# Reordering two seams of a long-convolution and token-mixing kernel: three phase steps ahead of the last inverse, plain products first in the second pass

## The chip, the cores and the metric

The kernel runs on one core of a Trainium2 chip. The metric is the device time of one execution in microseconds. Before the change it was 2134.84 us, the median of three runs (2129.86 to 2135.28).

## What is computed

Two steps follow each other. The first is a causal convolution of `x` (8 batches, 5696 positions, 128 channels) with a filter `h` of the same length. The second turns each value into a real and an imaginary part by a learned phase, mixes all positions with two 5696 x 5696 matrices, and ends in a small layer over the channels.

```python
L = 2 * S
y = irfft(rfft(x, n=L, axis=1) * rfft(h, n=L, axis=0), n=L, axis=1)[:, :S, :]
theta = y @ w_theta
zr, zi = y * cos(theta), y * sin(theta)
m = einsum('ts,bsd->btd', w_tok_r, zr) + einsum('ts,bsd->btd', w_tok_i, zi)
u = y + m
out = u + maximum(u @ w_ch, 0.0)
```

## The kernel before

**Convolution.** Batches go in pairs and channels in halves, which makes eight groups. Each group runs a forward transform (`stage_a`, `stage_b`) and an inverse (`stage_c`, `stage_d`); the forward part of one group is woven with the inverse of the one before (the loop at L594). `stage_b` writes the products with the filter's spectrum into `u_t` and `v_t` (L307), for which it loads filter chunks `hs` from HBM (L298). `stage_c` multiplies from these two tiles (L323, L324) and evacuates to `g`; `stage_d` multiplies `g` (L346), evacuates to `yt` on ScalarE (L349), and stores to `yt_hbm` (L355). For the last group the first half of `yt` is also copied straight into the tile `ya1` by SP (`load_ya1`, L549), and the rest is stored by GpSimd.

**Phase steps.** `phase_step` (L556) takes 128 positions of half the batches. It transposes them on TensorE (L569), forms the phase in PSUM (L399 to L405), copies the transposed values (L574), takes an absolute value and two sines on ScalarE (L410 to L412), multiplies twice on VectorE (L423, L424), and stores the values to `y2_hbm` (L575) and the two parts `zz` to `z_hbm` (L441) or straight into a `b` tile (L437). There are 22 steps for the first half of the batches (`steps0`) and 22 for the second (`steps1`). Of the first 22, ten are woven into the last group's `stage_c`, six into its `stage_d`, and six follow. Six of the woven steps also release one weight load each (`with_load`).

**Mixing.** Positions 0 to 5631 of both sides are cut in four halves of 2816. A pass `p` takes one half of the source positions. Within a pass, a pair `tt` of 128-row tiles is multiplied with the source tiles `b` in stretches of three (the source half is 11 tiles `j`, so a pair has four stretches: tiles 0 to 2, 3 to 5, 6 to 8, and 9 and 10). Most pairs use seven products in place of eight, as in Strassen's scheme (L1060), which needs sums of the `b` tiles (`sum_ops`, L642, five per tile) and of the weights (`w_sum`, L711). A few pairs use the eight plain products instead (L982), which need neither; `plain(p, tt)` names them. The pair called `None` is the last 64 rows (L934, L936), here "the short pair". The order of the pairs is the list `pairs` (L447): in the first pass the short pair stands next to last, in the second pass it stands first.

**Weights.** GpSimd loads the mixing matrices in chunks into a ring of six slots (`load_w`, L501); each load is four DMAs. `ring["upto"]` holds how far the loads may go, and `pump` issues them when a slot has been read. VectorE transposes each chunk into a `wt` tile (L702, `w_t`). `prepare(i + 1)` emits the transposes and sums of the next stretch ahead of the products of this one. At the end of a pair they are given out in steps between the products (`woven`), if the next pair isn't the short one.

**Order.** The instructions are put into a queue for each engine by a planner that follows program order and expected readiness; `tc.issue_after(x)` keeps the enclosed instructions behind `x` on the same engine. In two regions VectorE keeps the written order (`manual_schedule`, L894): at the start of each pass, up to `(0, 2, 6)` and up to `(1, 1, 0)`.

**Start of the passes.** For the first pass `b` tiles 0 to 8 are filled in part from `z_hbm` (L639) and in part straight from the phase steps; tiles 9 and 10 are loaded by SP in `open_mixing` (L680). The first stretches (`i == 1`) are interleaved with `steps1`, one step after every second piece. The values that a pair's result is added to, `cs`, come from `addend` (L801): for the first pass from `y2_hbm` (L814) or `yt_hbm` (L810), by SP, and for the first pair they are loaded behind the last `b` tile (`sides["late"]`). For the second pass `start_pass(1)` loads all eleven `b` tiles through ScalarE's queue (L628), each as soon as the last pair of the first pass has read its tile, and adds two small tiles `zl` (L835). Results of the second pass go through an output stage, `u_stage` (L773): transposes (L782), a product (L789) and a last VectorE operation (L791). `aside` gives these stages out, one per stretch, in two parts.

Of the kernel before, what the change touches and what calls it, by code (L numbers as in the profile page):

```python
# [22 lines left out]
def kernel(  # L23
# [310 lines left out]
    def stage_d(st, bp, dh, then=None):  # L334
        def chunk(n0, cn):
            if n0 == 0:
                st["yt"] = fg.tile([P, NB, N2], BF16, tag="yt", name="yt")
            g_, yt = st["g"], st["yt"]
            ps = psum()
            nq = 5 if cn == CN else cn  # L340
            for j in range(cn):
                n = n0 + j
                o = ps[:, j // nq, (j % nq) * NB:(j % nq + 1) * NB]
                for ri in range(2):
                    e_ = e_t[:K1, n, ri, :] if n < EN else e_t[:K1, N2 - n, ri, ::-1]
                    nc.tensor.matmul(o, g_[:K1, ri * N2 + n, :], e_, start=(ri == 0), stop=(ri == 1))  # L346
            y_out = yt[:, :, n0:n0 + cn].rearrange("p m (a q) -> p m a q", q=nq)
            y_in = ps[:, :cn // nq, :nq * NB].rearrange("p a (q m) -> p m a q", q=nq)
            nc.scalar.activation(y_out, y_in, AF.Copy)  # L349
            if n0 + cn == N2:  # L350
                if then is not None:
                    then(yt)
                for e in range(2):
                    t0 = H if then else 0
                    (nc.gpsimd if then else nc.sync).dma_start(  # L355
                        yt_hbm[dh * HD:(dh + 1) * HD, 2 * bp + e, t0:],
                        yt[64 * e:64 * e + 64].rearrange("p m n -> p (m n)")[:, t0:])
        return [lambda n0=n0, cn=cn: chunk(n0, cn) for n0, cn in CHN]

    zz_n, ZB = [0], 3  # L360
# [312 lines left out]
    def open_mixing():  # L673
# [170 lines left out]
    def prepare(i, at_once=True):  # L844
# [45 lines left out]
    nxt, second, st = None, None, {}  # L890
    ordered = ExitStack()
    for i, (k, p, tt, j0, s0, nj) in enumerate(stretches):
        if (p, tt, j0 + s0) in ((0, 0, 0), (1, None, 0)):
            ordered.enter_context(tc.manual_schedule(engines={mybir.EngineType.DVE}))  # L894
        elif (p, tt, j0 + s0) in ((0, 2, 6), (1, 1, 0)):
            ordered.close()
# [18 lines left out]
        a, nxt = nxt, None if i == 1 else prepare(i + 1, not woven)  # L915
        if woven:
            nxt, step = nxt
        if tt is None:


            if first_of_pair:
                ps = [mps.tile([P, 512], F32, tag=f"m{q}", name=f"m{q}") for q in ((M2, M6) if p else (M3, M4))]
                cs = [addend(p, h, NT - 1, h, m=64) for h in range(2)]
            a1, a2, sa = a
            terms = (((a1, M2, a2, M7), (a1, M6, a2, M5)) if sa is None else
                     ((sa, M2, a2, M4), (a1, M3, sa, M5)))
            for j in range(nj):
                jj = j0 + s0 + j
                for r in range(2):
# [3 lines left out]
                    for h, (x0, q0, x1, q1) in enumerate(terms):  # L933
                        nc.tensor.matmul(ps[h][:64], x0[:, j, :64, r], b[q0],  # L934
                                         start=st_, stop=False)
                        nc.tensor.matmul(ps[h][:64], x1[:, j, :64, r], b[q1],  # L936
                                         start=False, stop=sp_)
            if p == 1:
# [13 lines left out]
            continue  # L952
        classic = plain(p, tt)
        if first_of_pair and i:
            ms = [mps.tile([P, 512], F32, tag=f"m{q}", name=f"m{q}") for q in (range(7) if not classic else (M7, M5, M1, M3) if p else (M2, M6, M1, M7))]
# [10 lines left out]
        def aside(first_of, second_of):  # L966
            nonlocal second
            if first_of and spread and (p == 1 or (tt > 0 and not end_of_pair)):
                where_bg["tags"] = ("c2", "c3") if j0 + s0 == TJ else ("red", "mag")
                _, first, second = spread.pop(0)  # L970
                with tc.issue_after(sides["late"].ins) if p == 0 and tt == 1 else ExitStack():
                    first()
                    if len(spread) > 1:
                        spread[1][0]()
            if second_of and second is not None:
                second()
                second = None

        def product(a, jj, j, n, hs):
            for r in range(2):  # L980
# [29 lines left out]
        if classic:  # L1010
# [112 lines left out]
```

## Time and profile before

| | |
|---|---|
| runs, median of three | 2134.84 us (2129.86 to 2135.28) |
| profiled execution, its own time | 2127.44 us |
| its span, first to last instruction | 2125.3 us |
| mean granted TensorE clock | 0.971 |
| VectorE, ScalarE, GpSimd busy | 75%, 32%, 43% |
| L1060, a Strassen product of 512 columns | 379 ns each, 1600 and 160 of them |
| L702, a transpose of a weight chunk | 523 ns each, 720 of them |
| L501, a weight DMA issued by GpSimd | 550 ns each, 1440 of them |

A group of the profile is one line of the kernel with its engine, operation and tile. A time for one instruction runs from its start to its end, and matmuls overlap, so the pace of TensorE is read from the starts. "Idle before" is the time that an engine waited ahead of an instruction, and the releaser is what ended the wait. The DMA share is the mean busy share of the core's 16 DMA engines, and it can stand above 1 where transfers overlap.

### The profile page before, as it was taken

What the parts mean: (1) busy time and instruction counts of PE and PEld (TensorE: products, weight loads), DVE (VectorE), ACT (ScalarE), POOL (GpSimd) and SP (SyncE); (2) the same over time, 40 slices, a digit from 0 to 9 for tenths busy, and PEclk for the clock granted to TensorE, in tenths of its full rate; (3) what the DMA queues carried; (4) which work ended last, traced back from release to release, by engine and by line L of the source; (5) the groups of instructions that cost most, each with busy time, mean ns of one, the idle gap of its engine ahead of it and who ended that gap; (6) DMA issues with size and microseconds to landing.
All of it is one profiled execution on the core that took longest, in us unless ns stands there. A gap on an engine that the chain in (4) does not pass through costs nothing.

```text
span 2125.3 us, 41308 instructions
## 1 busy us (share of the span) xinstructions
PE 1984.6 (93%) x15587; PEld 1112.7 (52%) x15765; DVE 1593.7 (75%) x2880; ACT 674.6 (32%) x997; POOL 908.1 (43%) x1661
## 2 busy tenths in 40 slices
PE   4788889787999999999999998999999999999998
PEld 3787888754444444444444443444444444444444
DVE  7767767776778888888886757677777777686867
ACT  5777877883232323332310000011111111111111
POOL 5301011237344536354556543444444454545450
PEclk8699999999999999999999999999999999999999
DMA  6457464989789989898999879777878787969693
GB/s 141 100 130 171 128 161 132 230 249 231 159 154 179 174 177 166 172 174 174 176 174 158 138 145 268 108 140 140 147 134 150 129 155 129 157 123 158 125 157 90
DMA packets 408264, 334.95 MB, mean 158 GB/s; under 512 B 85927, under 2 KB 358439, under 8 KB 407079
## 3 DMA queue, kind: packets, MB, share of 16 engines
q0 software_dynamic: 225952, 156.72, 52.1%
q1 hardware_dynamic: 176128, 164.05, 26.7%
q10 hardware_dynamic: 5984, 11.54, 1.5%
q8 instruction: 123, 2.02, 0.4%
q14 instruction: 77, 0.63, 0.1%
HBM read 377.11 MB, written 92.49 MB: 221 GB/s over the span
## 4 chain that ended last, share of the span: by engine, by line
PE 64%; DMA 3%; DVE 3%; issue 1%; POOL 1%; ACT 0%; DVEq 0%; ACTq 0%; POOLq 0%
PE m L1060 57%; PE m L982 2%; DMA b<-z_hbm 2%; DVE c L1067 1%; PE v L789 1%; PE utp L782 1%; POOL ring L501 1%; PE m L1064 1%; DVE wt L702 1%; DMA ring<-in_moe_w_tok_r_dram 1%; PE m L936 0%; PE m L934 0%; PE theta_ps L388 0%; PE tpz L730 0%; DMA ring<-in_moe_w_tok_i_dram 0%
## 5 line engine op out<-in xcount | busy, mean ns | idle before, releaser
L501 POOL DMA_DIRECT2D ring<-in_moe_w_tok_i_dram x720 | 388.9, 550 | 675.9 <-DVE wt L702 597.5
L501 POOL DMA_DIRECT2D ring<-in_moe_w_tok_r_dram x720 | 387.4, 551 | 154.4 <-DVE wt L702 83.4
L702 DVE STREAM_TRANSPOSE wt<-ring 128x384 f32<-128x384 f32 (+2 forms) x720 | 358.7, 523 | 109.8 <-PE m L1060 71.8
L1060 PE MATMUL m<-b,wt 128*128 128x512 bf16 x1600 | 384.5, 379 | 4.1 <-DVE wt L702 1.7
L1060 PEld LDWEIGHTS <-wt 128*128 128x128 bf16 x1804 | 176.1, 98 | 215.5 <-DVE wt L702 4.4
L1067 DVE TENSOR_TENSOR c<-c,m 128x512 f32<-128x512 f32 x412 | 265.4, 670 | 0.4 <-PE m L1060 0.4
L784 ACT ACTIVATE ring<-utp 128x512 bf16<-128x512 bf16 (+1 forms) x86 | 50.9, 592 | 608.7 <-PE utp L782 608.7
L323 PE MATMUL ps<-r_u,u_t 128*128 128x128 f16 x1024 | 131.8, 228 | 12.4 <-DVE u_t L307 11.8
L324 PE MATMUL ps<-r_v,v_t 128*128 128x128 f16 x1024 | 130.7, 228 | 0.1
L982 PE MATMUL m<-b,wt 128*128 128x512 bf16 x469 | 113.4, 389 | 10.7 <-DMA b<-zz 6.6
L779 ACT ACTIVATE ub<-c 128x512 bf16<-128x512 f32 (+1 forms) x90 | 56.2, 628 | 197.2 <-DVE c L950 115.5
L129 POOL DMA_DIRECT2D x<-in_x_dram x64 | 33.9, 536 | 188.9 <-PE ps L193 178.8
L323 PEld LDWEIGHTS <-u_t 128*128 128x128 f16 x1024 | 106.1, 104 | 13.8 <-DVE u_t L307 13.8
L324 PEld LDWEIGHTS <-v_t 128*128 128x128 f16 x1024 | 105.1, 103 | 2.8 <-DVE v_t L307 1.3
L305 ACT ACTIVATE xs<-ps 128x1024 f16<-128x1024 f32 x96 | 94.4, 1011 | 14.0 <-DVE v_t L307 6.1
L307 DVE TENSOR_TENSOR u_t<-xs,hs 128x1024 f16<-128x1024 f16 x96 | 69.7, 726 | 33.3 <-ACT xs L305 20.7
L193 PE MATMUL ps<-f_t,x 89*128 89x180 f16 x512 | 80.9, 310 | 11.0 <-ACT xs L305 8.4
L982 PEld LDWEIGHTS <-wt 128*128 128x128 bf16 x528 | 51.1, 100 | 71.9 <-issue 17.4
L211 PEld LDWEIGHTS <-w_t 64*128 64x128 f16 x3240 | 60.2, 102 | 37.4 <-issue 24.5
L193 PEld LDWEIGHTS <-x 89*128 89x128 f16 x512 | 72.8, 235 | 12.8 <-issue 12.3
L390 ACT ACTIVATE red<-theta_ps,magic 128x512 f32<-128x512 f32 (+1 forms) x46 | 31.6, 687 | 135.1 <-PE theta_ps L388 113.9
L732 ACT ACTIVATE ring<-tpz 128x512 bf16<-128x512 bf16 (+1 forms) x46 | 27.5, 597 | 135.9 <-PE tpz L730 120.6
(2889 smaller groups left out, 3857.4 us busy)
## 6 DMA issues: line engine op xcount, KB each, us to landing
ring<-in_moe_w_tok_r_dram POOLq DMA_DIRECT2D x352, 96.0 KB, 4.6
ring<-in_moe_w_tok_i_dram POOLq DMA_DIRECT2D x352, 96.0 KB, 4.9
ring<-in_moe_w_tok_r_dram POOLq DMA_DIRECT2D x352, 80.0 KB, 4.5
ring<-in_moe_w_tok_i_dram POOLq DMA_DIRECT2D x352, 80.0 KB, 3.9
hs<-hf_hbm SPq DMA_DIRECT2D x192, 128.0 KB, 3.2
cp_hbm<-c SPq DMA_DIRECT2D x88, 256.0 KB, 2.4
c<-cp_hbm SPq DMA_DIRECT2D x88, 256.0 KB, 4.4
out_dram<-c SPq DMA_DIRECT2D x88, 256.0 KB, 4.4
```

The lines of the kernel that those rows point to most:

```text
L193: nc.tensor.matmul(ps[:, i // 2, (i % 2) * 2 * K1:(i % 2 + 1) * 2 * K1], lhs(q + i), f1_t[:NB], start=True, stop=True)
L211: nc.tensor.matmul(ps[:, e, j * HD:(j + 1) * HD], w_t2[rows, c0 + j, N2 * (1 - ri):N2 * (3 - ri)], a_st["a"][rows, ri * K1 + c0 + j, :], s ...
L305: nc.scalar.activation(xs[:, :, :, :ck], ps, AF.Copy)
L307: nc.vector.tensor_tensor(uv[r][:, :, :, c0:c0 + ck], xs[:, :, :, :ck], hv[:, r:r + 1, :, :ck].to_broadcast([P, 2, HD, ck]), op=mult)
L323: nc.tensor.matmul(o, u_t[:, at:at + P], r_u, start=True, stop=False)
L324: nc.tensor.matmul(o, v_t[:, at:at + P], r_v, start=False, stop=True)
L501: nc.gpsimd.dma_start(wb[32 * i:32 * i + 32, :ng, :nj * 64], bass.AP(tensor=a.tensor, offset=a.offset + row0 * S + p * H + i * QR + j0 * 6 ...
L702: nc.vector.transpose(wt.rearrange("p j t r -> p (j t r)").bitcast(F32).rearrange("p (j g t) -> p g j t", j=TJ, g=4)[:, :ng, :nj], wb[:, : ...
L779: nc.scalar.activation(ub[:m].rearrange("p b d -> p (b d)"), c[:m], AF.Copy)
L982: nc.tensor.matmul(ms[n // 2 * 2 + h], a[n][:, j, :, r], bts_of[p][jj][n % 2 * 2 + h][:, r, :], start=(n % 2 == 0 and jj == 0 and r == 0), ...
L1060: nc.tensor.matmul(ms[q], a[q][:, j, :, r], bts[jj][q][:, r, :], start=(jj == 0 and r == 0), stop=(jj == NJ - 1 and r == 1 and q not in left))
L1067: nc.vector.tensor_tensor(c, z, ms[q], op=op)
```

## The change

It has six parts.

1. In the last group, three phase steps are put ahead of `stage_c`; nine are woven into it and five into `stage_d`. The weight loads go with the same steps as before.
2. The stores of the last `yt` by GpSimd are kept behind a one-element copy, `gate`, which reads the last element that the copy into `ya1` writes.
3. In `open_mixing` the addends of the first pair are loaded between `b` tiles 9 and 10, no longer behind tile 10.
4. At the end of the stretches that are interleaved with the phase steps, the limit of the weight ring is lifted and `pump` called after all of the products, and no longer at the start of the last quarter.
5. The second pass begins with its plain pair, then comes the short pair. The short pair uses three sets of weights, one of them a sum (`w_sum` of 64 rows), with the differences of the `b` tiles, as it does in the first pass. Two of the five sums per `b` tile (the differences) are formed beside the plain pair and the other three beside the short one; before, the short pair came first with three of them and the plain pair followed with the other two. The PSUM banks of both pairs change.
6. The plain pair's weights in the second pass can be prepared in steps, woven into the last pair of the first pass. The short pair of the second pass now gives out output stages (`aside`).

```diff
@@ stage_d
                 if then is not None:
                     then(yt)
+                if then is not None:
+                    gate = nc.gpsimd.tensor_copy(small(0, 1)[HD:HD + 1], sides["phases"][1][HD:HD + 1, 3, H - 1:H]).ins
                 for e in range(2):
                     t0 = H if then else 0
-                    (nc.gpsimd if then else nc.sync).dma_start(
...
+                    with tc.issue_after(gate) if then else ExitStack():
+                        (nc.gpsimd if then else nc.sync).dma_start(
...
-    pairs = (list(range(21)) + [None, 21], [None] + list(range(22)))
+    pairs = (list(range(21)) + [None, 21], [0, None] + list(range(1, 22)))
...
-        now = [with_load(steps0.pop(0), 2 < n < 9) for n in range(10)] if last else []
+        if last:
+            for _ in range(3):
+                steps0.pop(0)()
+        now = [with_load(steps0.pop(0), n < 6) for n in range(9)] if last else []
...
-        now = [steps0.pop(0) for _ in range(6)] if last else []
+        now = [steps0.pop(0) for _ in range(5)] if last else []
@@ open_mixing
-        for j in range(len(bts_of[0]), NJ):
-            load_b(0, j, bp, nc.sync)
+        load_b(0, NJ - 2, bp, nc.sync)
+        sides["cs"] = [addend(0, n, t, h) for n, (t, h) in enumerate(((0, 1), (22, 0), (0, 0), (22, 1)))]
+        load_b(0, NJ - 1, bp, nc.sync)
@@ prepare
-            return a1, a2, None if p else w_sum(a1, a2, add, nj, m=64)
+            return a1, a2, w_sum(a1, a2, add, nj, m=64)
...
-            a = [w_t(w11, s0, nj), w_t(w12, s0, nj), w_t(w21, s0, nj, pool=sp), w_t(w22, s0, nj, pool=sp)]
+            a = {}
+
+            def some(n):
+                if n in (0, 1):
+                    a[n] = w_t((w11, w12)[n], s0, nj)
+                elif n in (4, 5):
+                    a[n - 2] = w_t((w21, w22)[n - 4], s0, nj, pool=sp)
+            if not at_once and p:
+                return a, some
+            for n in range(6):
+                some(n)
@@ the loop over stretches
-        if (p, tt, j0 + s0) in ((0, 0, 0), (1, None, 0)):
+        if (p, tt, j0 + s0) in ((0, 0, 0), (1, 0, 0)):
...
-            terms = (((a1, M2, a2, M7), (a1, M6, a2, M5)) if sa is None else
-                     ((sa, M2, a2, M4), (a1, M3, sa, M5)))
+            terms = ((sa, M2, a2, M4), (a1, M3, sa, M5))
...
+            if p:
+                aside(False, True)
             if p == 1:
                 for j in range(nj):
-                    for op in sum_ops(bts[j0 + s0 + j])[:3]:
+                    for op in sum_ops(bts[j0 + s0 + j])[2:]:
                         op()
...
-            with tc.issue_after(sides["late"].ins) if p == 0 and tt == 0 else ExitStack():
-                cs = [addend(p, n, t, h) for n, (t, h) in enumerate(where)]
+            cs = (sides["cs"] if p == 0 and tt == 0 else
+                  [addend(p, n, t, h) for n, (t, h) in enumerate(where)])
...
                     if q == 3 and n == 0:
-                        ring["upto"] = len(queue)
                         nxt = prepare(2)
+            ring["upto"] = len(queue)
+            pump()
             continue
...
-                    for op in sum_ops(bts[j0 + s0 + j])[3:]:
+                    for op in sum_ops(bts[j0 + s0 + j])[:2]:
                         op()
```

More of the change, by code (lines that the diff above doesn't have):

```diff
@@ L352, in chunk @@
                     then(yt)
+                if then is not None:
+                    gate = nc.gpsimd.tensor_copy(small(0, 1)[HD:HD + 1], sides["phases"][1][HD:HD + 1, 3, H - 1:H]).ins
                 for e in range(2):
                     t0 = H if then else 0
-                    (nc.gpsimd if then else nc.sync).dma_start(
-                        yt_hbm[dh * HD:(dh + 1) * HD, 2 * bp + e, t0:],
-                        yt[64 * e:64 * e + 64].rearrange("p m n -> p (m n)")[:, t0:])
+                    with tc.issue_after(gate) if then else ExitStack():
+                        (nc.gpsimd if then else nc.sync).dma_start(
+                            yt_hbm[dh * HD:(dh + 1) * HD, 2 * bp + e, t0:],
+                            yt[64 * e:64 * e + 64].rearrange("p m n -> p (m n)")[:, t0:])
         return [lambda n0=n0, cn=cn: chunk(n0, cn) for n0, cn in CHN]
@@ L917, with aside @@
             nxt, step = nxt
+        def aside(first_of, second_of):
+            nonlocal second
+            if first_of and spread and (p == 1 or (tt > 0 and not end_of_pair)):
+                where_bg["tags"] = ("c2", "c3") if j0 + s0 == TJ else ("red", "mag")
+                _, first, second = spread.pop(0)
+                with tc.issue_after(sides["late"].ins) if p == 0 and tt == 1 else ExitStack():
+                    first()
+                    if len(spread) > 1:
+                        spread[1][0]()
+            if second_of and second is not None:
+                second()
+                second = None
         if tt is None:
+            if p:
+                aside(True, False)
             if first_of_pair:
-                ps = [mps.tile([P, 512], F32, tag=f"m{q}", name=f"m{q}") for q in ((M2, M6) if p else (M3, M4))]
+                ps = [mps.tile([P, 512], F32, tag=f"m{q}", name=f"m{q}") for q in ((M1, M7) if p else (M3, M4))]
                 cs = [addend(p, h, NT - 1, h, m=64) for h in range(2)]
             a1, a2, sa = a
-            terms = (((a1, M2, a2, M7), (a1, M6, a2, M5)) if sa is None else
-                     ((sa, M2, a2, M4), (a1, M3, sa, M5)))
+            terms = ((sa, M2, a2, M4), (a1, M3, sa, M5))
             for j in range(nj):
@@ L937 @@
                                          start=False, stop=sp_)
+            if p:
+                aside(False, True)
             if p == 1:
                 for j in range(nj):
-                    for op in sum_ops(bts[j0 + s0 + j])[:3]:
+                    for op in sum_ops(bts[j0 + s0 + j])[2:]:
                         op()
@@ L954 @@
         if first_of_pair and i:
-            ms = [mps.tile([P, 512], F32, tag=f"m{q}", name=f"m{q}") for q in (range(7) if not classic else (M7, M5, M1, M3) if p else (M2, M6, M1, M7))]
+            ms = [mps.tile([P, 512], F32, tag=f"m{q}", name=f"m{q}") for q in (range(7) if not classic else (M3, M4, M5, M2) if p else (M2, M6, M1, M7))]
         if first_of_pair:
@@ L962 @@
         if j0 + s0 == (3 if classic else 2) * TJ:
-            with tc.issue_after(sides["late"].ins) if p == 0 and tt == 0 else ExitStack():
-                cs = [addend(p, n, t, h) for n, (t, h) in enumerate(where)]
[L966 to L977, printed above, removed]
+            cs = (sides["cs"] if p == 0 and tt == 0 else
+                  [addend(p, n, t, h) for n, (t, h) in enumerate(where)])
         def product(a, jj, j, n, hs):
```

## The prediction

> **What bounds the kernel now.** I read the page first, then busy time by stretch, then the waits and the order of time at the two places that the change touches.
>
> ```profile
> PE 1984.6 (93%) x15587; PEld 1112.7 (52%) x15765; DVE 1593.7 (75%) x2880; ACT 674.6 (32%) x997; POOL 908.1 (43%) x1661
> ```
>
> TensorE is busy 93% of 2125.3 us, so some 140 us of idle is all that reordering can win. Where it lies, by stretch (columns: us, then busy us of PE, PEld, DVE, ACT, POOL, then granted clock, DMA share, GB/s):
>
> ```profile
> 387.00:394.00 7.00, 1.05 (x21) 0.82 (x15) 4.30 (x8) 3.17 (x5) 5.91 (x11) 0.66 0.91 198
> 394.00:442.00 48.00, 43.34 (x634) 38.25 (x643) 35.14 (x57) 41.37 (x72) 10.17 (x22) 0.94 0.98 240
> 442.00:456.00 14.00, 8.26 (x76) 6.02 (x75) 12.57 (x25) 11.91 (x22) 4.41 (x9) 0.81 0.90 219
> 456.00:512.00 56.00, 49.95 (x398) 29.52 (x405) 40.43 (x76) 37.50 (x63) 44.19 (x81) 0.99 0.94 275
> 512.00:545.00 33.00, 23.66 (x99) 10.05 (x100) 20.26 (x35) 2.88 (x5) 17.84 (x33) 0.84 1.08 210
> 545.00:1283.00 738.00, 730.52 (x3629) 344.79 (x3699) 582.03 (x1135) 180.24 (x291) 379.02 (x697) 1.00 0.92 166
> 1283.00:1321.00 38.00, 28.67 (x120) 12.90 (x118) 32.22 (x60) 0.00 (x0) 9.22 (x18) 0.96 1.07 303
> 1321.00:1364.00 43.00, 41.32 (x204) 18.93 (x209) 22.49 (x41) 4.70 (x9) 17.17 (x32) 1.00 0.60 88
> ```
>
> The passes run at 99% (730.5 of 738). From 387 to 545, the change from convolution to mixing, 31.7 us are idle (158 less 126.3); from 1283 to 1321, where the second pass begins, 9.3. What ends the waits in the first place (us in total, times, longest):
>
> ```profile
> PE ps L323 <- DVE u_t L307: 5.3, 1, 5.3
> PE tpz L569 <- DMA ya<-yt: 3.4, 1, 3.4
> PE m L982 <- DMA b<-zz: 6.6, 2, 6.1
> PE m L1025 <- DMA yy<-y_hbm: 2.2, 1, 2.2
> SPq L628 <- DMA b<-zz: 10.5, 1, 10.5
> ```
>
> Why b<-zz came late stands in the order of time: the last store sat on POOL behind eight weight loads (507.23 to 511.6) and went out at 516.16, ten us after its product.
>
> ```profile
> 516.16 1.07 POOL L437 DMA_DIRECT2D b<-zz  x2 [3.08 <-DMA ring<-in_moe_w_tok_r_dram]
> 518.52 7.19 PE L982 MATMUL m<-b,wt 128*128 128x512 bf16 x24 [6.09 <-DMA b<-zz]
> ```
>
> At the second place the short pair (L934, L936) stands waiting for b tiles:
>
> ```profile
> 1289.61 0.38 PE L934 MATMUL m<-ring,wt 128*64 128x512 bf16 x1
> 1307.63 0.38 PE L936 MATMUL m<-b,wt 128*64 128x512 bf16 x1 [1.89 <-DMA b<-z_hbm]
> 1314.26 0.59 PE L936 MATMUL m<-b,wt 128*64 128x512 bf16 x1 [3.40 <-DMA b<-z_hbm]
> 1318.99 0.38 PE L936 MATMUL m<-b,wt 128*64 128x512 bf16 x1 [1.21 <-DMA b<-z_hbm]
> 1363.48 0.38 PE L1060 MATMUL m<-ring,wt 128*128 128x512 bf16 x1 [0.51 <-DVE wt L702]
> ```
>
> Matmuls of 512 columns start 0.2157 us apart here, so the short pair (8 per b tile, 11 tiles, and 2) needs 90 x 0.2157 = 19.4 us and took 31.3 (1289.6 to 1320.9); the pair of plain products (176 and 4) needs 38.8 and took 40.5. From 1289.6 to 1363.5 are 73.9 us.
>
> [...] after the 6.1 us wait, 24 matmuls took 7.19 us, where 24 x 0.2157 = 5.2; a wait costs more than its length. [...] with the DMA share at 1.07, b loads took 12.3 us (median) to land. [...] here 128x1024 takes 0.686 us, 0.617 from start to start, which I use.
>
> **The change, part by part.**
>
> Three phase steps ahead of the last inverse. A step is 1.1 us of PE (407.02 to 408.12), 1.78 of ACT (405.39 to 407.17), 1.8 of DVE (0.42 + 0.69 + 0.68), and three stores on SP (1.9 us). Their input landed by 376. ACT is idle for 5.53 us ahead of 395.70 and PE waits 5.3 ahead of 393.56 for the last u_t, so three steps (PE 3.3, ACT 5.3) fit. DVE has only 2.7 us free up to 394, so half of their 5.4 spills into the inverse; its first DVE copy is at 399.33. SP has nothing to issue from 393.1 to 401.9. The inverse and the stage after it then hold 14 steps instead of 16; ACT, busy 41.4 of 48 us, sets their pace: 2 x 1.78 = 3.6 if it stays so. I take 3 (0 to 3.6). The third step comes off the tail after the last yt copy; there the next late thing is the copy of yt into ya, landing at 451.9, so I count nothing for it.
>
> The gate on POOL. The two yt_hbm stores (2 x 64 rows x 5760 bytes, 0.74 MB) go only when the copy into ya has landed (5.4 and 5.6 us)[...]. Gain 0 to 2.5, I take 1. The gate itself is a one-element copy, by the nearest row (ring<-zz, L499) 0.18 to 0.58 us. Queued behind it on POOL are the stores and the half loads of b (L639), which waited 9.15 us until 452.64 anyway; that wait hides it. Each us that the copy lands after it costs one, 3 at most.
>
> Last stores ahead of weight loads. Two loads (8 DMAs, 507.2 to 511.6) move behind the last steps' stores, which can then go at 507 to 509. Gone are the 6.1 us wait and the 2.0 of cold clock. Next late are b tiles 9 and 10: their SP loads were held 10.5 us by that same store, and PE waited 0.9 for them at 526.63. It will want them at 512.4 + 5.2 = 517.6, and they should land about 520: some 2.5 us stay. The eight moved loads are first transposed at 526.7, so 2 us of delay are covered by 15. The addends' four loads go between b9 and b10: 1.5 to 4 us of SP (0.37 each undisturbed; 0.40 + 1.08 + 1.85 + 0.66 here) that delay b10, against the 2.2 us wait for yy. On paper 6.1 + 2.0 + 0.9 + 2.2 less 2.5 and less 2 is 6.7. But the share of DMA is 1.08 here, so what isn't waited for at one place may be at the next; I take 3 (-2 to 9).
>
> Sum of the first place: 3 + 1 + 3 = **7** (-3 to 13).
>
> Plain pair first in pass 2. No matmul is added: four products per tile and half in the short pair as before, sums in place of plain weights. PE starts at 1289.6 with work for 38.8 us instead of 19.4. It reaches tiles 3 at 1300, 6 at 1310, 9 and 10 at 1320.5 and 1321.3; before, 9 and 10 had landed by 1314.3 and 1319.0. The ring holds wider weights now, some 0.4 MB more by then, at 303 GB/s 1.3 us: a stall of 0 to 2. The plain pair's first weights are woven into the last stretch, w11 and w12 from loads long there; w21 and w22 land around 1290 by the 4.2 us of such loads and are wanted at 1289.6 + 24 x 0.2157 = 1294.8. So it ends at about 1329 to 1330.
>
> Then DVE. The sums are split 22 beside the plain pair and 33 beside the short one (before, the short pair had its 33 too, but stood first and waited for tiles anyway): 33 x 0.617 = 20.4 us, with eight transposes (2.2), four weight sums (0.25 to 0.35 each by L711), and four output stages at 0.68 that `aside` now starts here: 26.5 us beside PE's 19.4 + 4 x 0.86 = 22.9. DVE runs in written order, each stretch's preparation ahead of the sums of the one before, so it stays about one stretch behind PE: a stretch takes DVE 0.9 + 0.68 + 5.55 = 7.1, PE 5.2 + 0.86 = 6.1, and I reckon 1 us lost at two of the four stretches and 1.3 ahead of the first Strassen pair, whose weights VectorE has still to transpose. Start of that pair: 1329.5 + 22.9 + 2 + 1.3 = 1355.7 against 1363.5, **8** us earlier; two output stages more are then done (1.7), six sums more owed (3.7 of DVE, hidden in a pair where it is busy 74%). Bounds: 12 (all idle gone) and 3.
>
> Total 15 us. Against the profiled execution (2127.4 us, 2125.3 its span, 2.1 around it) that is 2112.4; it lies below the three timed runs, so I put it on their median: 2134.84 - 15 = **2120**.
>
> **Rivals.**
>
> A: DMA bounds the first place. For: shares of 0.90 to 1.08 from 387 to 545, the same bytes to move. Against: 210 to 275 GB/s there, 303 later, and 0.26 right after 550. Front 0, seam 8: 2127.
>
> B: the seam gives nothing, because wider weights and b tiles compete and DVE waits in order for w21. For: DMA 1.07. Against: 5 us of margin. Front 7: 2128.
>
> C, slower: DVE in written order becomes the bound of the short pair. An output stage's last operation (L791) stands ahead of the sums and waited 5.7 and 5.0 us for PE before. If DVE waits so in every stretch and PE then waits for the next weights behind those sums, a stretch takes 5.2 + 7.1 = 12.3 instead of 7: three such and a last one of 8 make 45 us instead of 26, the Strassen pair starts at 1374.8, 11.3 later than before. It decides when the next stretch's transposes stand behind the sums; as written they stand ahead, which speaks against it. 2139 with the front's 7, 2146 without; I put it at 2143.
>
> **How the numbers follow.** Forecast 0.57 (own range 2112 to 2126), A 0.18, B 0.13, C 0.12. Low end: both places near their best, 13 + 12, 2110. High end: 2133, over A and B with their spread and what C leaves out. About 0.3% (6.4 us) is what a measurement can tell from no change: below 2128.4 lie most of the forecast and of A and half of B, 0.72; between 0.18; above 2141.2 0.10.
>
> **What would show it.** Right: the wait of L323 for u_t shrinks to under 2 us with phase transposes in it; no 6 us wait for b<-zz near 512; PE idle from 387 to 545 down from 31.7 to about 25; the plain pair contiguous from the end of pass 1, waits for b<-z_hbm under 3 us in sum; short pair 24 to 27 us long. Wrong: PE waits for `wt` at the start of pass 2, gaps in the short pair beside a DVE at 100%, or POOL held by the gate after the half loads were due.

## The result, and the profile after

The changed kernel takes 2114.28 us, the median of four runs (2113.42 to 2116.9), beside 2132.35 us for the kernel before (2127.18 to 2135.28). The ratio is 0.992, with a 95% interval of 0.9896 to 0.9944: 17 us faster (12 to 22). In the experiments below the kernel before was run again many times, with medians of 2128.8 to 2130.4, so 14.5 to 16 us is the steadier figure. The changed kernel itself was timed in these four runs alone, so a difference of 1 or 2 us from its 2114.3 says little. The profiled execution took 2114.66 us, its span was 2112.9 us and its mean clock 0.969.

The page's line of busy time, and busy time by stretch (columns: us, then busy us of PE, PEld, DVE, ACT, POOL, then granted clock, DMA share, GB/s):

```profile
PE 2000.1 (95%) x15765; PEld 1115.9 (53%) x15765; DVE 1593.8 (75%) x2884; ACT 674.1 (32%) x997; POOL 906.6 (43%) x1662
```

```profile
387.00:394.00 7.00, 5.05 (x77) 3.88 (x74) 5.06 (x8) 4.38 (x7) 5.36 (x10) 0.66 0.88 171
394.00:442.00 48.00, 42.30 (x618) 36.30 (x616) 35.84 (x59) 40.67 (x71) 10.30 (x23) 0.94 0.99 248
442.00:456.00 14.00, 10.04 (x102) 7.35 (x101) 13.25 (x27) 13.57 (x25) 2.47 (x5) 0.88 0.89 214
456.00:512.00 56.00, 47.40 (x371) 27.59 (x369) 38.91 (x72) 35.44 (x61) 44.65 (x83) 0.94 0.93 263
512.00:545.00 33.00, 31.20 (x158) 14.43 (x157) 22.58 (x40) 5.97 (x10) 18.91 (x36) 1.00 1.18 246
545.00:1283.00 738.00, 734.17 (x3692) 344.17 (x3691) 585.91 (x1144) 176.90 (x286) 378.77 (x698) 1.00 0.93 168
1283.00:1321.00 38.00, 38.00 (x178) 17.21 (x176) 22.25 (x43) 0.27 (x1) 16.40 (x31) 1.00 1.07 289
1321.00:1364.00 43.00, 39.84 (x198) 17.86 (x196) 38.92 (x73) 5.83 (x11) 17.62 (x34) 0.96 0.73 120
```

From 387 to 545 TensorE is now idle for 22.0 us (158 less 136.0), where it was 31.7. Most of that came from one row, 512 to 545: from 23.66 to 31.20 busy, with the DMA share *up* from 1.08 to 1.18. The row from 456 to 512 went the other way, from 49.95 to 47.40. (The rows are fixed times, and the last inverse starts at 396.71 in this trace, at 393.56 in that of before, so a row doesn't hold quite the same work.) From 1283 to 1321 it has no idle time at all, at the same DMA share of 1.07. The last row shows the price: VectorE is busy for 38.92 of 43 us there (22.49 before), and TensorE has 3.2 us of idle time.

The order of time around the last stores. Columns: start, us, engine, line, instructions, and in brackets the wait ahead with its releaser.

```profile
510.33 1.08 POOL L440 DMA_DIRECT2D b<-zz  x2
511.40 2.19 POOL L504 DMA_DIRECT2D ring<-in_moe_w_tok_r_dram  x4
```

```profile
505.40 11.10 PE L1000 MATMUL m<-b,wt 128*128 128x512 bf16 x43 [3.31 <-DVE wt L709]
516.81 5.99 PE L1000 MATMUL m<-b,wt 128*128 128x512 bf16 x27 [0.30 <-DMA b<-zz]
527.92 1.02 PE L1000 MATMUL m<-b,wt 128*128 128x512 bf16 x4 [0.48 <-DMA b<-z_hbm]
```

The last store of z stood behind eight weight loads and went out at 516.16. It now goes at 510.33, ahead of them, and the wait of 6.09 us for b<-zz has become 0.30. (In the other nine traces with early stores such a wait is 3.41 us at most.) The wait of 2.23 us for an addend is gone. What comes next is small: 1.02 us for weights and 0.48 us for a b tile. One wait ahead of them grew, 3.31 us for weights, where 1.43 had been; it lies anywhere from 0.5 to 3.9 us in the other traces, whatever was edited.

The start of the second pass on TensorE:

```profile
1283.08 1.03 PE L1000 MATMUL m<-ring,wt 128*128 128x512 bf16 x4
...
1322.25 0.41 PE L963 MATMUL m<-ring,out__18429 128*64 128x512 bf16 x1
...
1346.04 0.62 PE L978 MATMUL m<-zl,ring 128*64 128x512 bf16 x2
1348.40 1.03 PE L1079 MATMUL m<-ring,wt 128*128 128x512 bf16 x2 [1.75 <-DVE wt L709]
1349.22 1.91 PE L1079 MATMUL m<-b,wt 128*128 128x512 bf16 x4
1350.93 1.06 PE L1079 MATMUL m<-ring,wt 128*128 128x512 bf16 x2
```

The plain pair runs without a wait from 1283.08 to 1322.25 (in the other kernels with this order and the same sums in the pair, its waits come to 0 to 2.7 us), the short pair until 1346.65 (24.4 us), and the first Strassen product comes 65.3 us after the pass began (73.9 before). It waits 1.75 us for weights, and then TensorE runs at half pace for some us, called a cold clock here: four products take 1.71 us (1349.22 to 1350.93), 0.43 apart in place of 0.2157, at a granted clock of 0.50. The first twelve take 4.29 us (1348.40 to 1352.69, granted clock 0.60), where 12 x 0.2157 is 2.59.

**Distances.** The last inverse starts somewhere between 392.3 and 397.6 us in the fourteen profiled kernels, whatever was edited. So I compare distances within a trace, from the start of one instruction to that of another, and leave out of the last two rows the three kernels that put sums later (below).

| distance, us | without the part | with it |
|---|---|---|
| first product of the last inverse to the last yt copy (steps ahead) | 47.9, 48.0, 48.1 | 46.3 to 48.3, mean 47.5 of eleven |
| last yt copy to first Strassen product (addends and stores) | 135.4, 136.0, 136.9 | 127.5 to 129.4, mean 128.7 of nine |
| first Strassen product of pass 1 to that of pass 2 (seam) | 786.0, 788.7 | 777.5 to 780.7, mean 779.0 of nine |
| from there to the last product whose weights come straight from a `wt` tile | 747.1, 747.3 | 747.8 to 749.7, mean 748.6 of nine |

By the means, the first place gave 0.5 + 7.4 us and the seam, the start of the second pass, 8.4, of which 1.4 was given back in the rest of the pass: 14.9 us in all. Each kernel has one trace. Within a cell the values differ by up to 3 us (786.0 and 788.7 for the same order of pairs), so the large entries are good to 1 or 2 us.

### The profile page after: what moved, and what is told of

It is laid out like the page before. It is cut to its first block, busy times and chain, and to the rows that moved or that the text cites. A ratio compares the mean times of both kernels' runs of the same rounds, so it can differ in the third digit from the quotient of the medians.

```text
span 2112.9 us, 41491 instructions
## 1 busy us (share of the span) xinstructions
PE 2000.1 (95%) x15765; PEld 1115.9 (53%) x15765; DVE 1593.8 (75%) x2884; ACT 674.1 (32%) x997; POOL 906.6 (43%) x1662
## 3 DMA queue, kind: packets, MB, share of 16 engines
q1 hardware_dynamic: 176128, 164.05, 27.1%
## 4 chain that ended last, share of the span: by engine, by line
PE 67%; DVE 3%; DMA 1%; issue 1%; POOL 0%; ACT 0%; DVEq 0%
PE m L1079 61%; PE m L1000 2%; DVE b L650 1%; PE v L796 1%; PE utp L789 1%; PE m L1083 1%; DVE c L1086 1%; DVE wt L709 1%; PE m L963 0%; PE m L965 0%; PE tpz L737 0%; PE theta_ps L391 0%; POOL ring L504 0%; DMA ring<-in_moe_w_tok_r_dram 0%; DMA wl<-in_moe_w_tok_i_dram 0%
```

## The experiments

All were timed beside the kernel before. My theory was the one in the prediction: two independent gains, one at each place. Ratios are to the kernel before (the changed kernel: 0.992).

**The two places apart.** One kernel has parts 1 to 4 of the change, the other parts 5 and 6. The edit of the first, as it stands against the changed kernel (with all that belongs to the short and the plain pair of pass 2); the second keeps this line and undoes parts 1 to 4:

```diff
-    pairs = (list(range(21)) + [None, 21], [0, None] + list(range(1, 22)))
+    pairs = (list(range(21)) + [None, 21], [None] + list(range(22)))
```

> Parts 1 to 4 alone (steps ahead, gate, addends between the b tiles, stores ahead of weight loads); the second pass starts with the short pair as before. Theory (the two places add up): the first Strassen product starts at about 571 us instead of 577.5, the stretch from there to the end of the first pass stays 712 us, the second pass's start takes 73.9 us as before, total about 6 us faster than before (ratio 0.997). Rival (what is won at the first place is given back later, because the DMA engines are full there): the first Strassen product starts early but the total stays within 2 us of before.

> Parts 5 and 6 alone (plain pair first in the second pass); the first place is as before. Theory: first Strassen product at about 577.5 us as before, the start of the second pass takes 65 to 66 us instead of 73.9, some 2.5 us of that come back in the first pair after it (cold clock), total about 6 us faster (ratio 0.997). Rival (what is won at the start of the second pass depends on the first place too, for instance on output stages and weights being in another phase): less than 3 us.

Measured: parts 1 to 4 alone 2123.84 us (2118.9 to 2125.21), ratio 0.9965 [0.9952, 0.9978]; parts 5 and 6 alone 2120.09 us (2116.4 to 2125.39), ratio 0.9954 [0.9939, 0.9968]. The product of the two ratios is 0.9919, the ratio of the whole 0.992. Both places gain, and within the intervals (some 3 us to each side) the two add up. Beside the kernel before, 2130.4 us in these rounds, the gains are 6.6 us, as forecast, and 10.3, where 6 was forecast. How the gain at the seam divides between part 5 and part 6 was not tried.

**Without the steps ahead.** Part 1 undone:

```diff
-        if last:
-            for _ in range(3):
-                steps0.pop(0)()
-        now = [with_load(steps0.pop(0), n < 6) for n in range(9)] if last else []
+        now = [with_load(steps0.pop(0), 2 < n < 9) for n in range(10)] if last else []
```

> The changed kernel with part 1 undone: ten steps in the last inverse and six in the stage after it, none ahead. Theory of the prediction (three steps in the gap shorten the inverse): 3 us slower than the changed kernel, last copy of yt about 3 us later than its 443.4. Rival, from the trace after (the last copy of yt came 1.9 us later with the steps ahead, and the copy into ya, not the steps, sets the start of the second half): within 1 us of the changed kernel, last copy of yt at 441 to 442.5, first phase step of the second half at 451 either way.

Measured: 2114.47 us (2112.77 to 2117.18), ratio 0.9925 [0.9912, 0.9938]. The forecast of 3 us failed, that of the rival held: the steps ahead are worth nothing that shows. Yet TensorE's wait for u_t is back:

```profile
PE ps L323 <- DVE u_t L307: 5.1, 1, 5.1
```

The changed kernel's trace tells why filling that wait won nothing. VectorE's last u_t and ScalarE's first activation of a step ahead there:

```profile
394.78 0.40 DVE L307 TENSOR_TENSOR u_t<-xs,hs 128x256 f16<-128x256 f16 x1 [1.71 <-DMA hs<-hf_hbm]
395.83 0.60 ACT L413 ACTIVATE mag<-ps 128x512 f32<-128x512 f32 x1 [3.46 <-DVE ring L577]
```

Only TensorE's part of the steps went into the gap. Their copies on VectorE stand behind u_t, which waits for filter chunks, so ScalarE still idles for 3.46 us and does most of the three steps inside the inverse. Busy time from the first product of the last inverse to the last yt copy, in the changed kernel and without the steps ahead (columns as above):

```profile
396.71:443.42 46.71, 40.99 (x616) 35.43 (x614) 35.45 (x57) 41.21 (x73) 10.24 (x22) 0.96 0.97 246
```

```profile
395.58:443.68 48.10, 43.39 (x631) 38.35 (x642) 34.87 (x57) 40.88 (x70) 11.14 (x23) 0.93 0.97 240
```

TensorE has 2.4 us less to do there, but ScalarE and VectorE have no less: 41.21 and 35.45 us, 40.88 and 34.87 without.

**Without the gate.** Part 2 undone; the stores of yt go at once:

```diff
-                    gate = nc.gpsimd.tensor_copy(small(0, 1)[HD:HD + 1], sides["phases"][1][HD:HD + 1, 3, H - 1:H]).ins
...
-                    with tc.issue_after(gate) if then else ExitStack():
```

> The changed kernel with one part undone: the stores of the second half of yt go out on GpSimd at once and not behind the one-element copy that waits for the load of ya. Theory [...]: the copy lands 1 to 1.5 us later after the last copy of yt, and the time is 1 us above the changed kernel's 2114.3. Rival (the stores are too small beside what else is under way, or the earlier stores make the loads of b earlier): no difference, within 0.5 us.

Measured: 2113.54 us (2112.59 to 2116.89), ratio 0.993 [0.9918, 0.9942]. The gate gains nothing that shows; the distance from the last yt copy to the first Strassen product is 128.5 us, amid the others. The traces tell why. First without the gate, then in the changed kernel (the last yt copy starts at 444.42 and 443.42):

```profile
454.74 0.29 PE L569 MATMUL tpz<-ident_bf,ya 128*128 128x128 bf16 x1 [3.27 <-DMA ya<-yt]
455.36 4.87 POOL L642 DMA_DIRECT2D b<-z_hbm  x9 [8.96 <-DMA z_hbm<-zz]
461.71 0.59 PE L997 MATMUL m<-b,wt 128*128 128x512 bf16 x2 [0.83 <-DMA b<-z_hbm]
```

```profile
451.07 0.29 PE L572 MATMUL tpz<-ident_bf,ya 128*128 128x128 bf16 x1 [2.07 <-DMA ya<-yt]
458.88 4.26 POOL L645 DMA_DIRECT2D b<-z_hbm  x8 [0.76 <-PE theta_ps L408]
463.98 1.49 PE L1000 MATMUL m<-b,wt 128*128 128x512 bf16 x4 [3.43 <-DMA b<-z_hbm]
```

With the gate the copy into ya is there 7.7 us after the last yt copy and not 10.3, a larger gain than the theory's 1 to 1.5. But GpSimd issues the half loads of b 15.5 us after the last yt copy and not 10.9, and TensorE waits 3.43 us for them, not 0.83. It is so in all traces: 7.5 to 8.9 and 15.5 to 16.2 us in the eleven with a gate, 10.3 to 10.5 and 10.9 to 11.2 in the three without. What is won at ya is lost at b.

**Without the early addends, without the early stores, and without both.** Part 3 undone, part 4 undone, then the two together:

```diff
-            cs = (sides["cs"] if p == 0 and tt == 0 else
-                  [addend(p, n, t, h) for n, (t, h) in enumerate(where)])
+            with tc.issue_after(sides["late"].ins) if p == 0 and tt == 0 else ExitStack():
+                cs = [addend(p, n, t, h) for n, (t, h) in enumerate(where)]
```

```diff
                     if q == 3 and n == 0:
+                        ring["upto"] = len(queue)
                         nxt = prepare(2)
-            ring["upto"] = len(queue)
-            pump()
             continue
```

> The changed kernel with one part undone: the four addends of the first plain pair are again loaded late, behind the stores, instead of ahead of the last b. Theory: the wait of 2.2 us for the addends (yy<-y_hbm at the last matmuls of the pair) comes back, and the time is 1 to 2 us above the changed kernel's 2114.3. Rival (the four addends only trade places with the last b, and take from it what they save): within 0.5 us or a gain, with the wait for b shorter by what the wait for yy is longer.

> The changed kernel with one part undone: in the first plain pair of pass 1 the weight loads of the third stretch are again queued on GpSimd ahead of the last stores of z. Theory (the weight loads had pushed the stores back, and the stores end the wait for the last b): TensorE waits 4 to 6 us for b<-zz near 512 us again, the first Strassen product comes 3 to 5 us later after the first products of the last inverse, and the time is 3 to 5 us above the changed kernel's 2114.3. Rival (the transfers at this place are bound by the DMA engines, whatever their order on the queue): within 1 us.

> The changed kernel with two parts undone at once: the weight loads again ahead of the last stores, and the four addends again loaded late. Undone alone they cost 9.6 and 5.0 us over the changed kernel's 2114.3. Theory (they are two ends of one wait: both bring the last stores and the last b earlier, and with the weight loads ahead of the stores an early addend helps nothing, since TensorE comes to it late): 6 to 9 us above the changed kernel, no more than with the weight loads undone alone. Rival (two separate waits): the two add up, 13 to 15 us above it.

Measured: late addends 2119.25 us (2115.81 to 2123.65), ratio 0.9954 [0.9942, 0.9966]; weight loads ahead of the stores 2123.92 us (2118.8 to 2128.48), ratio 0.9975 [0.9963, 0.9988]; both 2123.02 us (2122.15 to 2125.81), ratio 0.9966 [0.9954, 0.9979]. The distances from the last yt copy to the first Strassen product are 133.0, 134.7 and 136.9 us. GpSimd and TensorE with the weight loads ahead:

```profile
509.46 2.20 POOL L504 DMA_DIRECT2D ring<-in_moe_w_tok_r_dram  x4
511.63 2.18 POOL L504 DMA_DIRECT2D ring<-in_moe_w_tok_i_dram  x4
...
517.89 0.54 POOL L440 DMA_DIRECT2D b<-zz  x1 [0.74 <-DMA ring<-in_moe_w_tok_r_dram]
```

```profile
522.57 1.44 PE L1000 MATMUL m<-b,wt 128*128 128x512 bf16 x3 [6.08 <-DMA b<-zz]
```

The last store goes out at 517.89, behind the weight loads, and a wait of 6.08 us is back. With only the addends late, TensorE waits for one of them instead:

```profile
527.18 0.59 PE L1043 MATMUL m<-yy,ident_bf 128*128 128x512 bf16 x1 [2.52 <-DMA yy<-y_hbm]
```

Over 2114.3 the times are 5.0, 9.6 and 8.7 us longer. The forecasts for the two alone were 1 to 2 and 3 to 5, both too low, and why is not shown; that for both was 6 to 9. The two costs don't add up, in time (8.7 together, where the sum is 14.6) or in distance (8.2, where 4.3 and 6.0 make 10.3), which fits one shared wait and not two separate ones. From the side of the gain: with part 3 alone the distance shrinks by 1.4 us (136.1, the mean without both, to 134.7), no more than the three traces without both differ among themselves; with part 4 alone by 3.1, with both by 7.4. So each seems worth more when the other is there, on one trace for each. The medians of the kernels with late stores (2120.1 to 2123.9) are too close to rank.

**The lag at the end of the short pair.** The rest is about the 1.75 us wait for weights and the cold clock behind it. The wait is in eleven of the twelve traces with the new order of pairs, 1.75 us long in the changed kernel's and about 2.0 in the others (0.28 in the one with earlier sums, next). The cold clock is in four of these eleven only. Two with the same wait, without the gate and without the steps ahead:

```profile
1351.45 0.38 PE L1076 MATMUL m<-ring,wt 128*128 128x512 bf16 x1 [1.98 <-DVE wt L706]
1351.66 1.03 PE L1076 MATMUL m<-b,wt 128*128 128x512 bf16 x4
```

```profile
1351.38 0.63 PE L1076 MATMUL m<-ring,wt 128*128 128x512 bf16 x1 [1.99 <-DVE wt L706]
1351.81 1.91 PE L1076 MATMUL m<-b,wt 128*128 128x512 bf16 x4
```

Of the nine traces in the last row of the table, the three with a cold clock took 749.4 to 749.7 us for the rest of the pass, the six without 747.8 to 748.2. So what an edit could win here for certain is the wait, about 2 us; the cold clock, some 1.5 us more, follows it in some runs only.

First the sums, three beside the plain pair and two beside the short one:

```diff
-                    for op in sum_ops(bts[j0 + s0 + j])[2:]:
+                    for op in sum_ops(bts[j0 + s0 + j])[3:]:
...
-                    for op in sum_ops(bts[j0 + s0 + j])[:2]:
+                    for op in sum_ops(bts[j0 + s0 + j])[:3]:
```

> The changed kernel with a third sum per b tile (b11 + b22, which overwrites nothing) formed beside the plain pair, so that 33 sums stand there and 22 beside the short pair. Theory (VectorE in written order paces the short pair and makes TensorE wait 1.75 us for wt at 1348, after which it runs cold): the waits for wt in the short pair and after it go, the short pair is 1 us shorter and the first Strassen pair 2 to 3 us, total 3 to 4 us faster than the changed kernel. Rival (VectorE waits in the plain pair for weight loads, 5.4 and 5.5 us, so more sums there only move the lag): the short pair starts with VectorE further behind, total within 1 us of the changed kernel or slower.

Measured: 2115.64 us (2113.01 to 2121.35), ratio 0.9935 [0.9921, 0.995]. The wait at the first Strassen product fell to 0.3 us, but the plain pair has a new one, since VectorE is late with its last weights. The rival was right, the lag only moved:

```profile
1320.50 3.63 PE L1000 MATMUL m<-b,wt 128*128 128x512 bf16 x15 [2.97 <-DVE wt L709]
```

Then the stall at VectorE's start: in the changed kernel it stands 4.47 us for the small tiles zl, with the first transposes behind. The sum of those tiles moves to the start of the short pair:

```diff
-            nc.vector.tensor_add(zl[2], zl[0], zl[1])
...
+                if p:
+                    nc.vector.tensor_add(zl[2], zl[0], zl[1])
                 cs = [addend(p, h, NT - 1, h, m=64) for h in range(2)]
```

> The changed kernel with the sum of the two halves of the left rows (zl[0] + zl[1], which only the Strassen pairs read) moved on VectorE from the start of pass 2 to the start of its short pair. Theory (VectorE works in the written order there and stands 4.5 us for the load of zl, so the first transposes of weights come late, the ring's next loads are issued late, and everything behind lags into the first Strassen pair, whose first product waits 1.7 us for wt): the wait for wt at the first Strassen product goes, with the cold clock behind it, and the time is 2 to 4 us below the changed kernel's 2114.3. Rival (the loads of the ring are bound by the DMA engines, whose share is 1.1 in these 40 us, so that they land no earlier however early they are issued): the idle time only moves to the next wait for the ring, within 1 us.

Measured: 2114.86 us (2114.16 to 2117.86), ratio 0.9935 [0.9923, 0.9947]. The rival was right. VectorE no longer waits for zl, and waits for the ring's loads instead, up to nearly the same time (the last of these transposes starts at 1309.41 in the changed kernel). TensorE's wait at the first Strassen product is still 1.98 us:

```profile
1296.12 0.58 DVE L709 STREAM_TRANSPOSE wt<-ring 128x384 f32<-128x384 f32 x1 [3.22 <-DMA ring<-in_moe_w_tok_i_dram]
1302.64 0.58 DVE L709 STREAM_TRANSPOSE wt<-ring 128x384 f32<-128x384 f32 x1 [5.94 <-DMA ring<-in_moe_w_tok_r_dram]
1308.62 0.58 DVE L709 STREAM_TRANSPOSE wt<-ring 128x384 f32<-128x384 f32 x1 [5.41 <-DMA ring<-in_moe_w_tok_i_dram]
```

Last, the order itself: the three sums beside the short pair one stretch later, alone and with zl moved too:

```diff
             if p == 1:
-                for j in range(nj):
-                    for op in sum_ops(bts[j0 + s0 + j])[2:]:
-                        op()
+                for op in st.pop("behind", ()):
+                    op()
+                st["behind"] = [op for j in range(nj) for op in sum_ops(bts[j0 + s0 + j])[2:]]
```

> The changed kernel with the three sums of b beside the short pair of pass 2 put one stretch later on VectorE (each stretch's sums behind the next stretch's products), so that the nine sums of the stretch before the last (5.5 us on VectorE) no longer stand ahead of the first Strassen pair's transposes of weights. No sum is needed before the stretch of the Strassen pair that reads it. Theory (VectorE's written order, and not the loads, makes TensorE wait 1.75 us for wt at the first Strassen product of pass 2 and start cold behind it): the wait falls under 0.5 us, and the time is 2 to 3 us below the changed kernel's 2114.3. Rival (VectorE has this work to do in any order; put later, it pushes back the second Strassen stretch's transposes and sums by as much, or the ring's loads are what is late): the wait moves on into the first Strassen pair, and the time is within 1 us.

> As the kernel with the later sums, and the sum of the left rows (zl) moved to the start of the short pair too. Theory (with the lag in VectorE's order gone at the end of the short pair, starting the transposes earlier at the start of the plain pair adds nothing): the same time as with the later sums alone, within 1 us. Rival (the two stalls add, so that only both edits free the lag): 1 to 2 us below it.

Measured: 2121.43 us (2120.5 to 2122.82), ratio 0.9957 [0.9944, 0.9969], and with zl 2124.45 us (2121.66 to 2128.82), ratio 0.9983 [0.9971, 0.9994]. Both are slower than the changed kernel, and for a reason of my own making. The last six sums now lay outside the region of written order, and the planner put two of them between the transposes of the plain pair, where they wait for the last b loads and everything on VectorE waits with them:

```profile
1309.98 0.69 DVE L650 TENSOR_TENSOR b<-b 128x1024 bf16<-128x1024 bf16 x1 [12.73 <-DMA b<-z_hbm]
```

TensorE lost 3.67, 1.45 and 1.17 us in the plain pair. So these two say nothing on the theory. The repaired version keeps all sums in the written order, puts a stretch's sums behind the pair's last additions, and lets the region reach one stretch further:

```diff
-        elif (p, tt, j0 + s0) in ((0, 2, 6), (1, 1, 0)):
+        elif (p, tt, j0 + s0) in ((0, 2, 6), (1, 1, TJ)):
```

> The changed kernel with the sums of b beside the short pair of pass 2 one stretch later, all of them in the hand-written order of VectorE, whose region reaches one stretch further (in the kernel with the later sums the last six lay outside it, and the planner had put them into the plain pair, where VectorE stood 12.7 us for the last b). The first Strassen pair's transposes now come before the nine sums of j = 6 to 8, and the second stretch's before the six of j = 9 and 10. Theory (VectorE's order makes TensorE wait 1.75 us for wt at the first Strassen product of pass 2 and run cold behind it): that wait falls under 0.5 us, no longer one takes its place, and the time is 2 to 3 us below the changed kernel's 2114.3. Rival (VectorE is full from the plain pair's end to the second stretch of the Strassen pair, and the same work in another order makes TensorE wait elsewhere, for the second stretch's weights or for the short pair's last additions): within 1 us.

Measured: 2117.83 us (2116.63 to 2121.3), ratio 0.9941 [0.9925, 0.9957]. My theory fell: no gain, by the medians 3.5 us slower. VectorE at that place:

```profile
1336.50 0.69 DVE L798 SCALAR_TENSOR_TENSOR c<-v,c 128x512 f32<-128x512 f32 x1 [4.45 <-PE v L796]
...
1343.87 5.50 DVE L650 TENSOR_TENSOR b<-b 128x1024 bf16<-128x1024 bf16 x9
1349.28 1.49 DVE L709 STREAM_TRANSPOSE wt<-ring 128x384 f32<-128x384 f32 x3
```

Without the sums between, VectorE ran ahead, reached the last operation of an output stage too early and stood 4.45 us for TensorE's part of it. The time saved was idled away (from 1317 to 1347 VectorE is busy for 22.8 us, 27.1 in the changed kernel), nine other sums again stood ahead of the transposes, and TensorE waited 2.0 and 2.7 us for weights, at the first and second stretch of the Strassen pair. From the first of these on, the pass took 751.8 us by the table's last row, more than in any of the nine traces there. No version was measurably faster than the changed kernel.

## Why the prediction was right

**The sum.** I forecast a gain of 15 us; the distances give 14.9, the medians against those later ones of before 14.5 to 16. That the first place comes out (7 forecast, 7.9 by the distances) is luck: the 4 us put down for the steps and the gate are worth 0.5 at most by the distances, and the addends and stores gave 4.4 more than was put down for them. The time forecast (2120) lies 6 above the median measured, since I took the gain off the median of three runs, 2134.84, which lay 4 to 6 us above the later medians of the same kernel.

**Steps ahead, 3 us: failed.** "ACT ... sets their pace: 2 x 1.78 = 3.6 if it stays so." The means differ by 0.5 us, and undoing the part changed no time. I had checked that ScalarE was free in the gap, and let half of VectorE's work spill into the inverse, but not asked when ScalarE's input would be there: a step's copy on VectorE comes before its activations, and VectorE was itself waiting for filter chunks. The sign that I named, the wait for u_t under 2 us, came true, and meant nothing.

**Gate, 1 us (0 to 2.5): the low end.** Undone, the time is 0.7 us lower, within the spread. With it the copy into ya came 2.6 us earlier (what slows the copy when the stores go at once is not shown), but not for nothing: I had written that the wait of GpSimd's half loads of b would hide the gate, and they went out 4.6 us later. The gate itself opened in time (451.07), but stores of the next phase steps then went out ahead of these loads.

**Addends and stores, 3 us (-2 to 9): right mechanism, sized too small.** The paper sum was 6.7, and I cut it to 3 because the DMA share was 1.08. It measured 7.4. Of the 2.5 us that I left for b tiles 9 and 10, 0.48 showed. Rival A, that the transfers bound this place, fell with it: TensorE gained 7.54 us from 512 to 545 while the share rose to 1.18, and with the weight loads put back ahead of the stores, the same bytes took 6.0 us of distance more. In the changed kernel's trace from 1283 to 1321 three queues took 46.4, 41.9 and 18.9% of the 16 engines' time, and TensorE had no idle time there. A share above 1 was no ground for such a discount: what counted here was which transfer went first, and the one that was waited for had been sent last.

**Seam, 8 us (3 to 12): right.** It measured 8.4, with the plain pair contiguous and a short pair of 24.4 us (24 to 27 forecast). The stall for w21 didn't come. The wait ahead of the first Strassen pair was 1.75 where I had 1.3. Missing in my sum was what follows: 1.4 us on average given back. In the changed kernel's own trace it is 2.6 (749.7 less 747.1), and 1.7 of that is the cold clock, twelve products in 4.29 us in place of 2.59. "A wait costs more than its length" held here, after 1.75 us of waiting; in seven other traces the pace stayed full after about 2.0 us at the same place. I had counted 1.7 us back for the two output stages done early; that didn't show, and why stays open.

**Rival C** was slower by VectorE's order in the short pair. In the changed kernel the sums fill the time in which the output stages would make VectorE wait, which is 1.51 us at most there. The repaired order shows C's mechanism at work when that cover is taken away: 4.45 us of waiting at such a stage, and by the medians a slower kernel.

**The missed 1 to 2 us at the seam** can't be had by the orders that I tried: earlier sums move the wait into the plain pair, an earlier start meets the loads, later sums meet the output stages. VectorE is busy for 38.92 of 43 us there, so little room is left; that no order exists is not shown.

## What to carry to other kernels

When two early transfers feed one consumer, take them as one edit: in the traces the early stores or the early addends alone were worth 3.1 and 1.4 us, together 7.4. Before counting a gain from filling a gap on one engine, follow the work's chain through the other engines: the phase steps filled a wait of 5.1 us and won nothing. When a transfer is held back for another, see what stands behind it on its queue: with the gate the half loads of b went out 15.5 us after the last yt copy, 10.9 without. In an engine whose work is kept in written order, as VectorE's was here, an operation that looks like load may be the cover of a later wait: 1.51 us at most at an output stage with the sums between, 4.45 without.

## What the runs showed of the hardware

A DMA share above 1 didn't bar a gain from order: with 1.18 in the changed kernel, TensorE was idle for 1.8 of 33 us, with 1.08 before for 9.3. At the start of pass 2 earlier transposes, which free the ring's slots, hardly brought loads forward: in the changed kernel, the one with zl moved and the repaired one, two ring loads in a row kept VectorE 5.4 to 6.5 us each, at a DMA share of 1.09, 1.10 (both from 1270 to 1320) and 1.10 (1277 to 1317). In the changed kernel GpSimd issued the first of these loads from 1292.36, released by one of four transposes that began at 1291.49, and the transpose that waits for it started at 1303.34. With zl moved the four began at 1286.89 and the waiting one started at 1302.64: 4.6 us earlier there brought 0.7 here.

A wait of one length doesn't fix what the clock does: after about 2.0 us of waiting at the same place TensorE ran at half pace in three traces (single products of 0.63 us) and at full pace in seven (0.38 us).
